# Leftover rows stacked by transfers, power-based guards and code products on GpSimd, in a spectral filter beside a product-key expert layer

## The chip, the cores and the metric

The kernel runs on one core of one Trainium2 chip. Its engines work side by side, each through its own instruction queue in order: TensorE (PE; its weight loads are listed apart as PEld), VectorE (DVE), ScalarE (ACT), GpSimd (POOL) and SyncE (SP), which here only issues DMA transfers. The metric is the time of one execution in microseconds on the device; the span in a profile is the part of it from the first to the last instruction.

## What is computed

`x` is 2048 tokens of 576 numbers, and `xn` its layer norm. The output is `x + A(xn) + B(xn)`:

```python
def _A_ref(x, w_r, w_i):                      # a filter in the frequency domain
    X = rfft2(x, axes=(-2, -1))               # over the 2048 tokens and the 576 columns
    return irfft2(X * (w_r + 1j * w_i), s=(S, D))

def _B_ref(x, w_q, k1, k2, u, v):             # 32 heads, 8 x 8 experts, the best key of each half
    q = einsum("nd,dhc->nhc", xf, w_q)        # w_q: 576 x 32 x 256
    s1, s2 = q[..., :128] @ k1.T, q[..., 128:] @ k2.T        # 8 scores each
    e = argmax(s1) * 8 + argmax(s2)           # one expert per token and head, its softmax weight is 1
    act = gelu(einsum("nd,nhkd->nhk", xf, u[e]))
    return einsum("nhk,nhk,nhkd->nd", 1, act, v[e])
```

## The kernel before

**Transform.** The 2048 tokens lie as 128 partitions by 16 tiles, so the token transform splits into a part of 64 points and one of 32. Each tile's 576 columns are folded into a sum half and a difference half of 289 columns (`folds`), of which 256 are the main columns and 33 are "leftovers". `dft128` multiplies both with the 64-point matrix `Rs` (scaled by the token's 1/sigma). float16 products need high and low parts: the main columns go to `AB` (high, low), and the leftovers to `ABL`, stacked three times on 99 partitions (33 low, 33 high, 33 high), so that one product does all three combinations. The stack is made beforehand: `folds` copies the 33 columns three times into `fl`, and PE repeats the work on 99 columns.

Then come 16 groups `g` of frequencies. `d_fwd(g)` does the column transform (12 products from `AB` and 2 from `ABL`), `s_fwd` the 32-point transform of a pair of groups, `s_mul` the filter weights `W` (loaded by `load_w`, scaled by `w_scale`), and `s_inv(g)` the inverse 32-point transform back into `AB` and `ABL`, again with the leftovers tripled through a copy `yl`. At the end, for 16 token tiles `t`, `d_inv(t)` does the inverse column transform and `fin` the 64-point one, adds the expert part (`CAT` times the high and low parts of `vS`, four products for each tile) and `x`, and stores.

**Experts.** `w_q` (18.9 MB, 32 transfers into the five buffers `w`) is folded with the keys as it arrives (`fold_part`), centred and split (`fold_end`, `fold_last`) into `MU` and `MUL`. In eight rounds `r` of 256 tokens, `x_t` loads and splits the transposed x (`xT`), `scores` does 28 products of 512 columns, takes the maximum over seven key differences, marks its place and multiplies the marks with a code of powers of two; `route` reduces the codes and forms the expert's one-hot parts; `combine` brings the coefficients into `CAT`.

**Guards.** So that float16 does not overflow, `allmax` finds the largest entry of a tensor (a transpose on PE, a maximum on DVE, a product on PE that broadcasts it) and scales by it. It serves `x_scale`, `uv_prep`, `w_scale` and `fold_scale`.

**Order.** The program text is only a list of operations, numbered as it is read, and matmuls of one stage are joined into operations of some 2000 array cycles. `ORDER` (line 134) gives the sequence in which all of them are issued, and `BANK` the PSUM bank of each tile; both were written by a planner. All instructions are issued at line 312, so the profile names the groups by their tiles: `Rs,A` is dft128's main part and `Rs,yl` its leftovers, `c,AB` and `c,ABL` are d_fwd and d_inv, `A,s` is s_fwd, `s,y` and `s,yl` are s_inv, `A,c` and `vS,MT` are fin, `MU,xT` and `MUL,xT` are scores, `w,KP` is fold_part, `c,wm`, `c,uv` and `c,mm_` are the transposes of `allmax`. `port` marks operations of DVE with more than one SBUF input and those of POOL with inputs; a marked POOL operation waits for the last marked DVE operation issued before it (line 315).

The functions that the change touches:

## Time and profile before

| | us |
|---|---|
| median of three runs | 209.82 (207.26 to 209.93) |
| the profiled execution | 209.11 |
| its span | 206.3 |
| PE busy | 195.5 (95%) |
| DVE busy | 172.8 (84%) |
| ACT busy | 120.7 (59%) |
| POOL busy | 97.6 (47%) |
| DMA moved | 43.4 MB, 210 GB/s on average |

The page has the busy time of each engine, the span in 40 slices (tenths of the slice), the chain of work that ended last, and groups of equal instructions with their total busy time, the mean duration of one in ns and the idle time of the engine just ahead of them. Matmul ends are modelled: they overlap, so a group's mean duration is longer than its share of PE. A timeline line gives start, duration, engine, operation and count.

### The profile page before, as it was taken

The page shows a single profiled execution, that of the slowest core. Times are in us where ns is not written, and L with a number is a line of the kernel's source. Part 1 is how long each engine was busy: PE and PEld are TensorE (multiplying, and loading weights), DVE is VectorE, ACT ScalarE, POOL GpSimd, SP SyncE. Part 2 cuts the span into 40 slices and gives each one's busy share as a digit, 9 for nine tenths or more (in the row PEclk, how much of TensorE's full clock was granted, in tenths as well). Part 3 has the DMA queues.
Part 4 walks back from the last instruction along what each step waited for, and adds up shares of the span by engine and source line. Part 5 has one row for each costly group of instructions (what it writes and reads, how often), then busy time and mean ns, then how long its engine had stood idle before and what let it go on. Part 6 is the DMA issues. An engine that isn't in the chain of part 4 may idle for free.

```text
span 206.3 us, 5748 instructions
## 1 busy us (share of the span) xinstructions
PE 195.5 (95%) x2239; PEld 134.3 (65%) x2239; DVE 172.8 (84%) x397; ACT 120.7 (59%) x272; POOL 97.6 (47%) x160
## 2 busy tenths in 40 slices
PE   7588999999998999999999999999999999999992
PEld 2388669786567658544556668565686667868850
DVE  2899898847485787659999999999999999999863
ACT  2799997842437629988686936608682432333400
POOL 4548464002250033179538227405176666959750
PEclk9999999999999999999999999999999999999999
DMA  6999899999999999554725502520000000123195
GB/s 209 394 416 420 308 381 412 403 407 374 376 380 410 335 371 318 176 178 129 280 67 174 211 0 79 165 102 5 0 3 0 0 3 0 62 114 118 65 362 206
DMA packets 14859, 43.39 MB, mean 210 GB/s; under 512 B 1904, under 2 KB 4720, under 8 KB 14576
## 3 DMA queue, kind: packets, MB, share of 16 engines
q1 hardware_dynamic: 14832, 43.03, 56.6%
q8 instruction: 17, 0.28, 0.6%
q14 instruction: 10, 0.08, 0.1%
HBM read 38.30 MB, written 4.72 MB: 209 GB/s over the span
## 4 chain that ended last, share of the span: by engine, by line
PE 84%; DMA 8%; DVE 4%; ACT 1%; issue 1%; POOL 1%; DVEq 0%; SPq 0%; ACTq 0%
PE banks L312 84%; DMA w<-in_wq_dram 6%; DVE A L312 2%; DMA XN<-in_x_dram 1%; DVE st L312 1%; DVE rr L312 1%; ACT t L312 0%; POOL A L312 0%; DVE AB L312 0%; POOL MUL L312 0%; DVE XN L312 0%; ACT rr L312 0%; POOL rr L312 0%; DVEq L1022 0%; ACT yl L312 0%
## 5 line engine op out<-in xcount | busy, mean ns | idle before, releaser
L312 PE MATMUL banks<-MU,xT 128*128 128x512 f16 x192 | 46.3, 379 | 0.0
L312 POOL TENSOR_TENSOR y<-t,t 128x289 f32<-128x289 f32 x32 | 21.5, 695 | 43.8 <-DVE t L312 21.6
L312 PEld LDWEIGHTS <-AB 128*128 128x128 f16 x400 | 33.9, 122 | 6.2 <-issue 1.9
L312 PEld LDWEIGHTS <-xT 128*128 128x128 f16 x224 | 21.3, 100 | 22.8 <-issue 0.9
L312 PE MATMUL banks<-c,AB 128*128 128x145 f16 (+1 forms) x384 | 35.1, 227 | 0.0
L312 POOL TENSOR_TENSOR xT<-xf,xT 128x640 f16<-128x640 f32 x16 | 22.8, 1433 | 24.4 <-DVE w L312 10.4
L312 DVE SCALAR_TENSOR_TENSOR t<-banks,wx,Wt 128x578 f32<-128x578 f32 x32 | 24.4, 812 | 7.1 <-PE banks L312 4.1
L312 POOL TENSOR_TENSOR A<-t 128x289 f32<-128x289 f32 x32 | 21.5, 694 | 7.0 <-DVE MT L312 3.8
L312 DVE TENSOR_TENSOR AB<-banks,AB 128x512 f16<-128x512 f32 x32 | 21.2, 675 | 1.8 <-ACT AB L312 1.7
L312 PE MATMUL banks<-Rs,A 64*128 64x128 f32 x256 | 18.6, 288 | 3.9 <-ACT Rs L312 2.9
L312 ACT ACTIVATE es<-banks,sc 128x290 f32<-128x290 f32 (+1 forms) x16 | 9.9, 625 | 18.9 <-PE banks L312 12.5
L312 PEld LDWEIGHTS banks<-Rs,A 64*128 64x128 f32 x256 | 16.5, 194 | 6.3 <-ACT Rs L312 4.6
L312 PE MATMUL banks<-w,KP 128*32 128x288 f32 x256 | 18.6, 412 | 1.3 <-DMA w<-in_wq_dram 1.2
L312 ACT ACTIVATE AB<-banks 128x512 f16<-128x512 f32 x32 | 18.4, 591 | 1.7 <-PE banks L312 1.2
L312 PE MATMUL banks<-c,ABL 99*128 99x289 f16 (+1 forms) x64 | 18.5, 290 | 0.0
L312 DVE TENSOR_REDUCE MT<-w 128x128 bf16<-128x896 bf16 (+1 forms) x16 | 18.2, 1140 | 0.1
L312 ACT ACTIVATE A<-banks 128x578 f32<-128x578 f32 x16 | 10.3, 645 | 13.1 <-PE banks L312 12.2
L312 PE MATMUL banks<-A,s 64*64 64x289 f32 x256 | 17.8, 410 | 0.0
L312 PE MATMUL banks<-s,y 64*128 64x128 f32 x256 | 17.4, 278 | 0.0
L312 ACT ACTIVATE ABL<-banks 99x256 f16<-99x256 f32 x32 | 11.6, 379 | 9.3 <-PE banks L312 8.8
L312 PEld LDWEIGHTS banks<-s,y 64*128 64x128 f32 x256 | 15.4, 187 | 2.1 <-issue 1.4
L312 DVE SCALAR_TENSOR_TENSOR XN<-banks,sc,XN 128x578 f32<-128x578 f32 (+1 forms) x18 | 12.9, 746 | 1.9 <-PE banks L312 1.9
(124 smaller groups left out, 359.9 us busy)
## 6 DMA issues: line engine op xcount, KB each, us to landing
w<-in_wq_dram SPq DMA_DIRECT2D x32, 576.0 KB, 6.9
xf<-in_xT_dram SPq DMA_DIRECT2D x16, 320.0 KB, 3.3
Wt<-in_W_dram SPq DMA_DIRECT2D x8, 578.0 KB, 6.6
out_dram<-XN SPq DMA_DIRECT2D x14, 288.0 KB, 2.4
s<-in_s_dram SPq DMA_DIRECT2D x16, 192.0 KB, 5.7
XN<-in_x_dram SPq DMA_DIRECT2D x2, 1156.0 KB, 12.6
XN<-in_x_dram SPq DMA_DIRECT2D x3, 578.0 KB, 5.8
c<-in_c_dram SPq DMA_DIRECT2D x1, 868.5 KB, 11.2
```

The lines of the kernel that those rows point to most:

```text
L312: o.last = fn(*[x.place() if isinstance(x, _Ps) else x for x in args], **{k: x.place() if isinstance(x, _Ps) else x for k, x in kw.items()})
```

## The change

- **Forward leftovers.** `folds` orders the columns so that 65 leftover columns of both halves lie side by side; `fl` and the copies go. `dft128` makes them once, high and low, in `HL`, and after the last tile `spread` fills the three rows of `ABL` with six transfers of 33 or 32 rows.
- **Inverse leftovers.** `s_inv` keeps the main columns. `s_left` does the leftovers of two groups in four quarters of the array and stacks them with six transfers; `s_last` does groups 14 and 15 as before, without transfers.
- In `d_fwd` and `d_inv` the leftover products come last and are operations of their own (`cut`).
- **Guards.** `root` replaces `allmax` except in `x_scale`: a sum of squares from ACT, one product on PE that adds over the partitions, and one DVE operation on the bit pattern that halves the exponent.
- **Codes.** Scores and codes lie with the seven differences outermost; the code product moves from DVE to POOL, and `route`'s reduction becomes three maxima.
- `CAT` holds high and low parts so that the low part of `vS` needs only half the rows; two such products of `fin` share the array. The tables `RT`, `_columns` halves and masks follow the new layouts, and `fold_last` writes chunk by chunk.
- `Rs` is scaled on POOL from tile 2 on; the statistics of tiles 10 and 14 move from DVE to ACT; three of four centrings in `fold_part` move from DVE to POOL; `EG` halves, so four of `d_inv`'s differences move from POOL to DVE. `y` and `es` share a buffer `U` with `HL`, and `y` gets four slots instead of two.
- `ORDER` and `BANK` are new throughout. In the new order on SP, two of spread's transfers stand ahead of the wq load numbered 331 and four behind it; on PE, the main products of groups 3, 0 and 1 come first, then that load's fold product, then the leftover product of group 1. The first `route` follows its code product at once on DVE; later ones have the next round's maximum and comparison between.

The diff, without `ORDER`, `BANK` and table construction:

```diff
+    def cut(self):
+        self.split = True
...
+    U = K([128, 2316], F32, "U")
+    slots["y"], slots["es"] = ([U[:, 579 * i:579 * i + 578] for i in range(4)], [U[:, 580 * i:580 * i + 580] for i in range(2)])
+    turn["y"] = turn["es"] = 0
+    HL = view(U, [64, 2, S], F16)
 
     ABg = AB.rearrange("p q c (g n) -> p q c g n", g=16)
     ABLg = ABL.rearrange("p b (g n) -> p b g n", g=16)
-    place = [8 * (g % 2) + g // 2 for g in range(16)]
+    place = [4 * (g % 4) + g // 4 for g in range(16)]
     ABt = AB.rearrange("p q c (n t) -> p q c n t", t=16)
     ABLt = ABL.rearrange("p b (n t) -> p b n t", t=16)
-    ABi = AB.rearrange("p q c (a g e m) -> p q (c a) g e m", a=2, g=16, e=2)
-    ABLi = ABL.rearrange("p b (a g e m) -> p (b a) g e m", a=2, g=16, e=2)
+    ABi = AB.rearrange("p q c (a e g m) -> p q (c a) g e m", a=2, g=16, e=2)
...
+    def root(src, k, dst, e):
+
+        p = PS("m", (128, 64))
+        P.matmul(p[:, :k], on[:, 0:1].to_broadcast([128, 128]), src, start=True, stop=True)
+        v = p[:, :k].bitcast(I32)
+        if len(dst.shape) == 3:
+            v = v.unsqueeze(2).to_broadcast([128, k, 2])
+        V.tensor_scalar(dst.bitcast(I32), v, 0.5, float(0x1FBD1DF5 + (e << 23)), op0=OP.mult, op1=OP.add)
+
+    SA = (3, 5, 7, 9, 10, 11, 13, 14, 15)
...
         xn = XN[:, t]
-        e = T([128, 2, L], F32, "e", 4, "A2")
-        G.tensor_tensor(e[:, 1], xn[:, 0:L], xn[:, L:], op=OP.subtract)
-        V.scalar_tensor_tensor(e[:, 0], xn[:, 0:L], rr[:, 2, t:t + 1], xn[:, L:], op0=OP.add, op1=OP.add)
+
+        e = T([128, 578], F32, "e", 4, "A2")
+        G.tensor_tensor(e[:, 0:256], xn[:, 31:287], xn[:, L + 31:L + 287], op=OP.subtract)
+        G.tensor_tensor(e[:, 256:287], xn[:, 0:31], xn[:, L:L + 31], op=OP.subtract)
+        V.scalar_tensor_tensor(e[:, 287:576], xn[:, 0:L], rr[:, 2, t:t + 1], xn[:, L:], op0=OP.add, op1=OP.add)
         Rs = T([128, 2, 64], F32, "Rs", 3)
-        A.activation(Rs, Rm, AF.Copy, scale=rr[:, 0, t:t + 1])
-        fl = T([128, 2, 3, 33], F32, "fl", 3, "yl")
-        if t in FG:
-            G.tensor_copy(fl, e[:, :, 0:33].unsqueeze(2).to_broadcast([128, 2, 3, 33]))
+        if t > 1:
+            G.tensor_scalar(Rs, Rm, rr[:, 0, t:t + 1], None, op0=OP.mult)
         else:
-            A.activation(fl, e[:, :, 0:33].unsqueeze(2).to_broadcast([128, 2, 3, 33]), AF.Copy)
-        FF[t] = (e, Rs, fl.rearrange("p b a k -> p b (a k)"))
+            A.activation(Rs, Rm, AF.Copy, scale=rr[:, 0, t:t + 1])
+        FF[t] = (e, Rs)
...
-        for b in range(2):
-            for h, r in enumerate(hs):
-                P.matmul(p[:99, h, 256 + 64 * b:320 + 64 * b], fl[r, b], Rs[r, 0], start=True,
-                         stop=True, tile_position=(64 * h, 0))
+        for h, r in enumerate(hs):
+            P.matmul(p[:65, h, 256:320], e[r, 256:321], Rs[r, 0], start=True, stop=True, tile_position=(64 * h, 0))
         m = p[:, :, 0:256].rearrange("p h (n r) -> p n h r", r=2)
-        l = p[:, :, 256:384].rearrange("p h (n r) -> p n h r", r=2)
+        l = p[:64, :, 256:320].rearrange("p h (n r) -> p n h r", r=2)
         hi, ab = (AB[:, q].rearrange("p c (h n) -> p (c h) n", n=64)[:, :, 4 * t:4 * t + 4].rearrange("p n (h r) -> p n h r", r=2)
                   for q in range(2))
         A.activation(hi, m, AF.Copy)
         V.tensor_tensor(ab, m, hi, op=OP.subtract)
-        lo = ABL.rearrange("p b (h n) -> p (b h) n", n=64)[:, :, 4 * t:4 * t + 4].rearrange("p n (h r) -> p n h r", r=2)
-        A.activation(lo[:99], l[:99], AF.Copy)
-        V.tensor_tensor(lo[:33], l[:33], lo[:33], op=OP.subtract)
+        lh, ll = (HL[:, q].rearrange("p (h n) -> p h n", n=64)[:, :, 4 * t:4 * t + 4].rearrange("p n (h r) -> p n h r", r=2)
+                  for q in range(2))
+        A.activation(lh, l, AF.Copy)
+        V.tensor_tensor(ll, l, lh, op=OP.subtract)
+
+    @staged
+    def spread():
+        for k, q in ((1, 0), (2, 0), (0, 1)):
+            for b, n in enumerate((33, 32)):
+                Q.dma_start(ABL[n * k:n * k + n, b], HL[31 * (1 - b):31 * (1 - b) + n, q])
...
-        V.tensor_reduce(uv[:, 0:1], uf, axis=AX, op=OP.max, apply_absolute_value=True)
-        V.tensor_reduce(uv[:, 1:2], vs, axis=AX, op=OP.max, apply_absolute_value=True)
-        allmax(uv[:, 0:2], 2, sc[:, 0:2])
+        for k, z in enumerate((uf, vs)):
+            A.activation(vS[:, 0, :z.shape[1]], z, AF.Square, accum_out=uv[:, k:k + 1])
+        root(uv[:, 0:2], 2, sc[:, 0:2], 1)
+        V.tensor_scalar(sc[:, 0:2], sc[:, 0:2], 1e-10, None, op0=OP.max)
...
-            if (b, s) == (3, 3):
-                V.tensor_reduce(mm_[:, 3 + h:4 + h], mt[b][:, h, :288], axis=AX, op=OP.max, apply_absolute_value=True)
...
+            A.activation(w[:, 0:2], mt[b][:, :, :288], AF.Square, accum_out=mm_[:, b:b + 1])
             V.tensor_scalar(c, c, -1.0 / 576, None, op0=OP.mult)
-            V.tensor_scalar(M, M, c, None, op0=OP.add)
+            (G if b < 3 else V).tensor_scalar(M, M, c, None, op0=OP.add)
             A.activation(MTL[:, b], M[:, 512:576].unsqueeze(1).to_broadcast([128, 2, 64]), AF.Copy)
-            if b < 3:
-                V.tensor_reduce(mm_[:, b:b + 1], M, axis=AX, op=OP.max, apply_absolute_value=True)
...
-        sv = p[:, :, :448].rearrange("p t (m e) -> p t m e", e=7)
+        sv = p[:, :, :448].rearrange("p t (e m) -> p t e m", e=7)
         mx = T([128, 2, 64], F32, "mx", 4)
-        V.tensor_reduce(mx, sv, axis=AX, op=OP.max)
+        V.tensor_reduce(mx, sv.rearrange("p t e m -> p t m e"), axis=AX, op=OP.max)
         wk = T([128, 2304], BF, "wk", 5, "w")
-        eq = wk[:, 0:896].rearrange("p (t m e) -> p t m e", t=2, e=7)
-        V.tensor_tensor(eq, sv, mx.unsqueeze(3).to_broadcast([128, 2, 64, 7]), op=OP.is_equal)
-        V.tensor_tensor(wk[:, 896:1792].rearrange("p (t n) -> p t n", t=2), wk[:, 0:896].rearrange("p (t n) -> p t n", t=2),
+        eq = wk[:, 0:896].rearrange("p (t e m) -> p t e m", t=2, e=7)
+        V.tensor_tensor(eq, sv, mx.unsqueeze(2).to_broadcast([128, 2, 7, 64]), op=OP.is_equal)
+        G.tensor_tensor(wk[:, 896:1792].rearrange("p (t n) -> p t n", t=2), wk[:, 0:896].rearrange("p (t n) -> p t n", t=2),
                         wt.unsqueeze(1).to_broadcast([128, 2, 448]), op=OP.mult)
...
-        wv = wk[:, 896:1792].rearrange("p (m e) -> p m e", e=7)
+        wv = wk[:, 896:1792].rearrange("p (t e m) -> p t e m", t=2, e=7)
...
-        V.tensor_reduce(v0, wv, axis=AX, op=OP.max)
+        V.tensor_tensor(wv[:, :, 4:7], wv[:, :, 4:7], wv[:, :, 0:3], op=OP.max)
+        V.tensor_tensor(wv[:, :, 3:5], wv[:, :, 3:5], wv[:, :, 5:7], op=OP.max)
+        V.tensor_tensor(v0.rearrange("p (t m) -> p t m", t=2), wv[:, :, 3], wv[:, :, 4], op=OP.max)
...
-        A.activation(chl[:, :, 0:64], ca, AF.Copy)
-        G.tensor_tensor(chl[:, :, 64:128], ca, chl[:, :, 0:64], op=OP.subtract)
+        c4 = chl.rearrange("p i (a e) -> p (i a) e", a=2)
+        A.activation(c4[:, 0:4:3], ca, AF.Copy)
+        G.tensor_tensor(c4[:, 1:3], ca, c4[:, 0:4:3], op=OP.subtract)
...
-            P.matmul(p[:, b, :L], ABLg[:99, b, place[g], :], dl[:99, b, :], start=True, stop=False)
             for c in range(2):
                 cs = slice(0, 145) if b == c else slice(145, 289)
                 for n, (ha, hb) in enumerate(((0, 0), (0, 1), (1, 0))):
-                    P.matmul(p[:, b, cs], ABg[:, ha, 2 * b + c, place[g], :], dc[:, b, hb, cs], start=False,
-                             stop=(c == 1 and n == 2))
+                    P.matmul(p[:, b, cs], ABg[:, ha, 2 * b + c, place[g], :], dc[:, b, hb, cs], start=(c == n == 0), stop=False)
+        plan.cut()
+        for b in range(2):
+            P.matmul(p[:, b, :L], ABLg[:(99, 96)[b], b, place[g], :], dl[:(99, 96)[b], b, :], start=False, stop=True)
...
-        yl = T([128, 2, 3, 33], F32, "yl", 3)
-        A.activation(yl, y[:, :, 128:161].unsqueeze(2).to_broadcast([128, 2, 3, 33]), AF.Copy)
-        Y[g] = (y, yl.rearrange("p r a k -> p r (a k)"))
+        Y[g] = y
 
     @staged
     def s_inv(g):
 
         p = PS("c", (128, 2, 4, 128))
-        (y, yl), s = Y.pop(g), S32.pop(g)[:, 192:]
-        for c in range(3):
+        y, s = Y[g], S32[g][:, 192:]
+        for c in range(2):
             for ri in range(2):
                 for e in range(2):
                     r = slice(64 * e, 64 * e + 64)
-                    pe = e ^ g % 2
-                    if c < 2:
-                        lt, po = y[r, ri, 161 * c:161 * c + 128], p[:, pe, c, :]
-                    else:
-                        lt, po = yl[r, ri], p[:99, pe, 2, :]
-                    P.matmul(po, lt, s[r, 64 * ri:64 * ri + 128], start=(ri == 0), stop=(ri == 1),
-                             tile_position=(64 * e, 0))
+                    P.matmul(p[:, e ^ g % 2, c, :], y[r, ri, 161 * c:161 * c + 128], s[r, 64 * ri:64 * ri + 128],
+                             start=(ri == 0), stop=(ri == 1), tile_position=(64 * e, 0))
         hi, ab = (ABi[:, q, :, g] for q in range(2))
         pv = p[:, :, 0:2].rearrange("p e c (b a m) -> p (c b a) e m", b=2, a=2)
         A.activation(hi, pv, AF.Copy)
         V.tensor_tensor(ab, pv, hi, op=OP.subtract)
-        lv = p[:99, :, 2].rearrange("p e (b a m) -> p (b a) e m", b=2, a=2)
-        lo = ABLi[:99, :, g]
-        A.activation(lo, lv, AF.Copy)
-        V.tensor_tensor(lo[:33], lv[:33], lo[:33], op=OP.subtract)
-
-
-    EG = range(0, 16, 2)
+
+    @staged
+    def s_left(g):
+        p = PS("c")
+        for ri in range(2):
+            for q in range(2):
+                y, s = Y[g + q], S32[g + q][:, 192:]
+                for e in range(2):
+                    r, o = slice(64 * e, 64 * e + 64), 64 * (e ^ q)
+                    P.matmul(p[o:o + 64, q, :128], y[r, ri, 128:192], s[r, 64 * ri:64 * ri + 128], start=(ri == 0),
+                             stop=(ri == 1), tile_position=(64 * e, o))
+        h = T([128, 2, 4, 64], F16, "lo", 2)
+        hi, lo = (h[:, n].rearrange("p c (q m) -> p c q m", q=2) for n in range(2))
+        pv = p[:, :, :128].rearrange("p q (c m) -> p c q m", c=4)
+        A.activation(hi, pv, AF.Copy)
+        V.tensor_tensor(lo, pv, hi, op=OP.subtract)
+        for k, n in ((1, 0), (2, 0), (0, 1)):
+            for e in range(2):
+                to = ABL[33 * k:33 * k + 33].rearrange("p b (a e n) -> p (b a) e n", a=2, e=2)
+                Q.dma_start(to[:, :, e, 32 * g:32 * g + 64], h[64 * e:64 * e + 33, n])
+
+
+    @staged
+    def s_last(g):
+
+        y, s = Y[g], S32[g][:, 192:]
+        yl = T([128, 2, 3, 33], F32, "lo", 2)
+        A.activation(yl, y[:, :, 128:161].unsqueeze(2).to_broadcast([128, 2, 3, 33]), AF.Copy)
+        p = PS("c")
+        for ri in range(2):
+            for e in range(2):
+                r = slice(64 * e, 64 * e + 64)
+                P.matmul(p[:99, e ^ g % 2, :128], yl[r, ri].rearrange("p a k -> p (a k)"), s[r, 64 * ri:64 * ri + 128],
+                         start=(ri == 0), stop=(ri == 1), tile_position=(64 * e, 0))
+        to = ABL[:99].rearrange("p b (a e g m) -> p (b a) g e m", a=2, e=2, g=16)[:, :, g]
+        pv = p[:99, :, :128].rearrange("p e (c m) -> p c e m", c=4)
+        A.activation(to, pv, AF.Copy)
+        V.tensor_tensor(to[:33], pv[:33], to[:33], op=OP.subtract)
+
+    EG = range(0, 16, 4)
...
+        for h in range(2):
+            for i in range(2):
+                r = slice(64 * i, 64 * i + 64)
+                P.matmul(ps[i][:, h, :L], CAT[r, t + i, :], vS[r, 1, L * h:L * h + L], start=False, stop=False,
+                         tile_position=(64 * i, 0))
         plan.pack = set()
         for i in range(2):
             for h in range(2):
-                for q in range(2):
-                    P.matmul(ps[i][:, h, :L], CAT[:, t + i, :], vS[:, q, L * h:L * h + L], start=False, stop=(q == 1))
+                P.matmul(ps[i][:, h, :L], CAT[:, t + i, :], vS[:, 0, L * h:L * h + L], start=False, stop=True)
...
+    spread()
...
+        if g > 13:
+            s_last(g)
+        elif g % 2:
+            s_left(g - 1)
         if g + 2 < 16:
             s_mul(g + 2)
         if g + 4 < 16:
             d_fwd(g + 4)
-            load_s32(g + 4)
             if g % 2 == 1:
+                load_s32(g + 3)
+                load_s32(g + 4)
```

80 lines of the change are left out of this document (44 added, 36 removed), and 127 rows, old and new, of tables (BANK, ORDER).

## The prediction

> **What bounds the kernel now.** I read the page first: its slices of the span and the chain.
>
> ```profile
> PE   7588999999998999999999999999999999999992
> DVE  2899898847485787659999999999999999999863
> DMA  6999899999999999554725502520000000123195
> PE 84%; DMA 8%; DVE 4%; ACT 1%; issue 1%; POOL 1%; DVEq 0%; SPq 0%; ACTq 0%
> ```
>
> TensorE (PE) is busy from the fifth slice on, VectorE (DVE) from the nineteenth, and the DMA engines are full for the first fifteen (a slice is 5.16 us). The chain in order of time:
>
> ```profile
> 22.65 6.62 DMA w<-in_wq_dram
> 29.32 27.28 PE banks L312 x407
> 56.61 6.03 DMA w<-in_wq_dram
> 62.68 139.31 PE banks L312 x1438
> ```
>
> and the engines by stretches (busy PE, PEld, DVE, ACT, POOL; clock, DMA share, GB/s):
>
> ```profile
> 10.00:20.00 10.00, 8.21 (x136) 7.87 (x137) 9.61 (x29) 10.00 (x29) 6.27 (x18) 1.00 1.02 420
> 30.00:40.00 10.00, 10.00 (x178) 8.90 (x176) 8.83 (x24) 8.00 (x21) 2.71 (x8) 1.00 1.03 412
> 105.00:120.00 15.00, 15.00 (x156) 9.42 (x157) 14.76 (x33) 11.66 (x21) 7.67 (x9) 1.00 0.41 135
> 165.00:180.00 15.00, 15.00 (x150) 10.69 (x149) 14.61 (x28) 4.69 (x11) 11.24 (x19) 1.00 0.06 22
> ```
>
> Three regimes. Up to about 30 us the normalisation is held by DVE and ScalarE (ACT), with the x and wq loads behind. From 30 to 202 us PE has no gap, although the wq loads fill the DMA to the fifteenth slice. In the late part DVE is within 2 or 3% of full, so it is a second bound just behind PE. Hence an edit is worth the PE time that it removes after 30 us, provided DVE falls by as much. The profiled execution took 209.1 us (span 206.3 and 2.8 around it), 0.7 under the median of 209.8; I sum against 209.1.
>
> **PE terms.** The rows:
>
> ```profile
> L312 PE MATMUL banks<-Rs,yl 64*99 64x64 f32 x128 | 7.5, 241 | 0.0
> L312 PE MATMUL banks<-s,yl 64*99 64x128 f32 x128 | 9.3, 269 | 0.0
> L312 PEld LDWEIGHTS banks<-A,s 64*64 64x64 f32 x256 | 9.9, 133 | 6.7 <-issue 1.3 <-ACT A L312 0.9 <-DVE w L312 0.4
> 30.00:40.00 10.00, 2.64 (x48) 2.51 (x48) 0.00 (x0) 1.34 (x4) 1.00 1.03 412
> 30.99 0.49 PE L312 MATMUL banks<-Rs,yl 64*99 64x64 f32 x8
> 31.31 1.18 PE L312 MATMUL banks<-Rs,A 64*128 64x128 f32 x16
> 42.29 0.27 PE L312 MATMUL banks<-c,wm 128*2 128x128 f32 x1
> 42.40 0.29 PE L312 MATMUL banks<-c,ABL 99*128 99x289 f16 x1
> 44.72 2.18 PE L312 MATMUL banks<-A,s 64*64 64x289 f32 x32
> 46.83 2.15 PE L312 MATMUL banks<-w,KP 128*32 128x288 f32 x32
> 65.19 1.04 PE L312 MATMUL banks<-s,yl 64*99 64x128 f32 x16
> 66.17 0.30 PE L312 MATMUL banks<-c,ABL 99*128 99x289 f16 x1
> 188.60 1.21 PE L312 MATMUL banks<-A,c 64*64 64x289 f32 x16
> 189.74 0.67 PE L312 MATMUL banks<-vS,MT 128*128 128x289 f16 x4
> 190.24 0.29 PE L312 MATMUL banks<-c,ABL 99*128 99x290 f16 x1
> ```
>
> A float32 matmul leaves two records. Ends are modelled, so I price a burst from its start to the next start.
>
> Forward leftovers (dft128): the 128 records become 64, because one product of 65 columns replaces two of 99. A tile's eight records take 31.31 - 30.99 = 0.32 us; halved, 0.16 less. Six of the 16 tiles (48 of 128 records) lie after 30 us: **-1.0**. The other ten save 1.6 that counts only where DVE and ACT let the front move; that is in the front's term below.
>
> Inverse leftovers (s_inv to s_left): 16 records take 66.17 - 65.19 = 0.98 us, that is 61 ns each and 7.8 us for 128. Afterwards 112 records run in four quarters of the array, as the s_fwd burst does: 32 records of 289 columns in 46.83 - 44.72 = 2.11 us, 66 ns each, 29 ns when scaled to 128 columns. The weight loads of that burst take 9.9/256 = 39 ns, which may be the floor. So 112 x 29 to 39 = 3.2 to 4.4, and s_last's 16 at 61 ns add 1.0: saved 2.4 to 3.6, taken **-2.8**, nearer the load row.
>
> Output (fin): four vS products take 190.24 - 189.74 = 0.50 us. The 32 that carry the low part become 32 of half height, two side by side: 32 x 125 ns = 4.0 becomes 2.0, **-2.0** (0 if the pairs do not overlap; the float32 rows of 64 partitions above do).
>
> Guards: ten transposes go (w_scale seven, uv one, fold_scale two) at 42.40 - 42.29 = 0.11 us each, **-1.1**; one matmul each stays. If a neighbour's fill hid them, 0. A DVE reduction goes with each; nothing waits longer.
>
> New switches of array layout: 16 records of fin's first step take 1.14 us from start to start, where sixteen at 66 ns would be 1.06. So leaving the quartered layout costs up to 0.1. s_left enters and leaves it seven times, s_last and fin's half-height products add some ten changes: 0 to 2.4, taken **+1.2**. The Trainium skill, TensorEngine Tiling (Array Packing), Key Properties, speaks against the change here: altering the tiling mode drains TensorE. It has no price; by that rule the term stays positive, and the trace's 0.08 us agrees.
>
> **The front.** The statistics of two more tiles (10 and 14) go from DVE to ACT, Rs goes to GpSimd (POOL), the tripled leftover copies vanish, and the low subtraction shrinks:
>
> ```profile
> L312 DVE BATCH_NORM_STATS2 st<-XN 128x6 f32<-128x288 f32 x18 | 7.2, 438 | 2.2 <-DMA XN<-in_x_dram 2.2
> L312 DVE TENSOR_TENSOR ABL<-banks,ABL 33x256 f16<-33x256 f32 x32 | 12.5, 406 | 1.5 <-ACT AB L312 0.8 <-ACT ABL L312 0.5
> ```
>
> DVE loses 2 x 2 x 0.438 = 1.8, and half of 16 x 0.406 at most, 3.2, since the elements per partition halve: up to 5 us on an engine that is 88 to 96% busy in the two early stretches above. ACT gains two tiles' statistics, but loses 14 of the Rs scalings. x still has to arrive, so I take **-2.0** (bounds 0 and -5), with the ten tiles above in it.
>
> Against that stands spread(): the leftovers reach ABL only through six transfers, three copies of 65 rows of 4 KB, 0.8 MB. At 412 GB/s that is 2.0 us on a full DMA. SP issues them in order among the wq loads: in the new order the last four stand behind one more wq load, and the leftover product of group 1 stands right after that load's fold product. Everything behind it on PE waits, then s_fwd and s_mul. The landing is bounded by
>
> ```profile
> w<-in_wq_dram SPq DMA_DIRECT2D x32, 576.0 KB, 6.9
> out_dram<-XN SPq DMA_DIRECT2D x14, 288.0 KB, 2.4
> ```
>
> 0 (three main products of d_fwd and folds cover it) to 6.9; four of the six are 0.53 MB, 1.3 us behind that load: **+1.5**. The 42 small transfers of s_left fall mostly in the empty DMA and are read only by the last matmul of d_inv. I cost them at nothing; if that cover goes, the last pair costs one landing, 2.4. Groups 14 and 15 avoid it through s_last. ACT, 8.00 of 10 busy from 30 to 40 us and less full later, takes the new squares at nothing.
>
> **DVE and POOL, late.**
>
> ```profile
> L312 DVE TENSOR_TENSOR w<-w,wt 128x896 bf16<-128x896 bf16 x8 | 5.3, 660 | 0.1
> L312 DVE TENSOR_REDUCE MT<-w 128x128 bf16<-128x896 bf16 x8 | 8.6, 1076 | 0.1
> L312 DVE TENSOR_TENSOR w<-w,MT 128x512 bf16<-128x512 bf16 x16 | 6.5, 416 | 0.1
> L312 DVE SCALAR_TENSOR_TENSOR t<-banks,sc,es 128x288 f32<-128x288 f32 x8 | 4.1, 514 | 0.7 <-POOL A L312 0.5 <-ACT es L312 0.2
> L312 POOL TENSOR_TENSOR xT<-xf,xT 128x640 f16<-128x640 f32 x16 | 22.8, 1433 | 24.4 <-DVE w L312 10.4 <-DVE wt L312 4.5 <-DVE wx L312 3.6
> 98.73 1.54 DVE L312 TENSOR_TENSOR w<-MT,iv 128x512 bf16<-128x512 bf16 x1
> 105.65 0.42 DVE L312 TENSOR_TENSOR w<-MT,iv 128x512 bf16<-128x512 bf16 x1
> 98.58 1.40 POOL L312 TENSOR_TENSOR xT<-xf,xT 128x640 f16<-128x640 f32 x1 [0.88 <-ACT xf L312]
> ```
>
> DVE loses the code product (5.3), 16 low subtractions of s_inv for 9 (2.8), and gets three maxima of 384, 256 and 128 elements for each reduction; on the line through 512 and 896 elements (0.09 us and 0.64 ns an element) they take 0.76 against 1.08, 2.5 in all. The strided maximum and the comparison keep their element counts: nothing, with 1 us either way. EG halves, so four differences return from POOL to DVE: +2.1. Sum -8.5, above the 4.7 that PE saves late, so DVE stays behind PE: no term. POOL takes 8 products of 896 elements, at 1433/640 = 2.24 ns about 2.0 us each, 16 in all, on 50 to 75% busy.
>
> **Sum:** -1.0 - 2.8 - 2.0 - 1.1 + 1.2 - 2.0 + 1.5 = -6.2, so 202.9; **203.0 us**. Its own range is 199 to 207.
>
> **Rivals.**
> 1. *The front swallows it* (207.6). Scores cannot start before the wq stream ends, in the fifteenth slice, and spread's 2.0 us lengthen that stream. If PE runs dry before it, only late savings count: ten of 16 groups' leftovers -1.8, fin -2.0, guards -0.7, switches +1.0, and +2.0: -1.5, 207.6. For: the DMA share of 1.03. Against: PE has no gap from 30 us and several groups to draw on.
> 2. *DVE waits for POOL* (216.6, slower). Each route needs its code product from POOL, and it can sit behind an xT difference. The 98.73 row starts inside POOL's 98.58 operation, ends just after it, and takes 1.54 instead of 0.42. If DVE stands 2.0 us for each of eight products, that is 16 - 8.5 = +7.5 on an engine that is 98% busy. It eats PE's gain from 0.5 us of standing per product ((8.5 - 4.7)/8), and the kernel gets slower beyond 1.1. Against: in the new order the route after the first has another round's maximum and comparison between product and use. The Trainium skill, SBUF — State Buffer, Who interferes with whom, has the rule: a DVE operation with two SBUF inputs and a GpSimd operation that reads SBUF exclude each other for a whole instruction. The 98.73 row agrees.
> 3. *The front was the bound* (198.4). If the relief of DVE before 40 us comes through whole (-5) and spread hides (0): 209.1 - 1.0 - 5 - 2.8 - 2.0 - 1.1 + 1.2 = 198.4. For: DVE and ACT are at 9.61 and 10.00 of 10 from 10 to 20 us. Against: the DMA share of 1.02 there.
>
> **Numbers.** Forecast 0.58, rival 1 0.22, rival 2 0.10, rival 3 0.10. A measurement of this kernel tells about 2% from no change: 205.6 and 214.0. A tenth of the forecast case lies above 205.6: faster 0.52 + 0.10 = 0.62, same 0.28, slower 0.10. The range 197 to 210 leaves out rival 2 and the edges of 1 and 3.
>
> **What would show it.** Right: s_left records near 35 ns, no s,yl product outside groups 14 and 15, PE without gaps from 40 us, DVE clearly under PE late. Wrong: a wait of PE on a transfer into ABL at 40 to 50 us above 3 us (rival 1 when the wq stream then ends late), or route maxima that start long after the operation before them, released by POOL (rival 2). PE gaps late with DVE full would break the premise that PE is what ends last.

## The result: 3.7% slower

The changed kernel takes 216.57 us (214.67 to 217.34), the kernel before 208.69 (207.26 to 209.93): ratio 1.037, 95% interval 1.026 to 1.048. The forecast was 203.0, with 197 to 210 as its range. The profiled execution took 217.34 us (span 215.2). Its slices, in the order PE, DVE, clock, DMA:

```profile
PE   7678797994799999799999999999999999999990
DVE  3859859370046166378495899999999996999883
PEclk9979999999589999999999999999999999999999
DMA  6999899899987999875875203416012100005476
```

PE, nearly without a hole from the fifth slice on before, now has holes up to the seventeenth (a slice is 5.4 us), the deepest in the tenth; from there it is full as before. So the loss lies in the first 92 us. Three rows from PE's timeline of the kernel before (last burst of `dft128`, first of scores, last of `fin`), then the same places in the changed kernel:

```profile
37.27 0.83 PE L312 MATMUL banks<-Rs,yl 64*99 64x64 f32 x16
...
83.86 1.03 PE L312 MATMUL banks<-MU,xT 128*128 128x512 f16 x4
...
201.55 0.67 PE L312 MATMUL banks<-vS,MT 128*128 128x289 f16 x4
```

```profile
40.01 1.56 PE L324 MATMUL banks<-Rs,A 64*128 64x128 f32 x28 [0.41 <-POOL Rs L324]
...
96.96 1.90 PE L324 MATMUL banks<-MU,xT 128*128 128x512 f16 x8
...
209.12 1.03 PE L324 MATMUL banks<-vS,MT 64*128 64x289 f16 x8
```

Scores start 13.1 us later (96.96 - 83.86), and the stretch from there to the last product is 5.5 us shorter (209.12 - 96.96 = 112.2 against 117.7). The difference is the 7.6 us that PE ends later. The late part is what the change was expected to bring; the front ate it and more.

Where PE stands still between 44 and 62 us, on PE and on SP's queue:

```profile
49.00 0.69 PE L324 MATMUL banks<-w,KP 128*32 128x288 f32 x8 [0.33 <-DMA w<-in_wq_dram]
49.62 0.94 PE L324 MATMUL banks<-c,AB 128*128 128x145 f16 x12
52.38 0.69 PE L324 MATMUL banks<-w,KP 128*32 128x288 f32 x8 [1.82 <-DMA w<-in_wq_dram]
54.87 1.71 PE L324 MATMUL banks<-c,ABL 99*128 99x289 f16 x6 [1.79 <-DMA ABL<-U]
```

```profile
42.64 1.26 SPq L324 DMA_DIRECT2D ABL<-U  x2
43.99 0.52 SPq L324 DMA_DIRECT2D w<-in_wq_dram  x1
44.57 3.17 SPq L324 DMA_DIRECT2D ABL<-U  x4
...
54.14 2.11 SPq L324 DMA_DIRECT2D w<-in_wq_dram  x4
```

`ABL<-U` are the transfers of `spread`. PE waits first for the wq load that was issued at 43.99 between them (it lands at 52.38, 8.4 us later), then for the rows themselves (issued until 47.74, there at 54.87). The next four wq loads go out at 54.14. By the profile it isn't a fold on PE that holds them: SP's waits just before end when the wq load lands (1.9 us) and then when rows of `spread` do. Its waits for such rows in the whole run (total, times, longest):

```profile
SPq L324 <- DMA ABL<-U: 1.6, 4, 0.6
```

### The profile page after: what moved, and what is told of

It is laid out like the page before. It is cut to its first block, busy times and chain, and to the rows that moved or that the text cites. A ratio compares the mean times of both kernels' runs of the same rounds, so it can differ in the third digit from the quotient of the medians.

```text
span 215.2 us, 5686 instructions
## 1 busy us (share of the span) xinstructions
PE 195.1 (91%) x2165; PEld 127.2 (59%) x2165; DVE 155.9 (72%) x379; ACT 115.4 (54%) x258; POOL 121.5 (56%) x184
## 5 line engine op out<-in xcount | busy, mean ns | idle before, releaser
L324 POOL TENSOR_TENSOR U<-t,t 128x289 f32<-128x289 f32 x32 | 21.7, 696 | 34.5 <-DMA xf<-in_xT_dram 23.3
L324 PE MATMUL banks<-Rs,A 64*128 64x128 f32 (+1 forms) x320 | 21.9, 289 | 7.1 <-POOL Rs L324 4.0
L324 PEld LDWEIGHTS banks<-Rs,A 64*128 64x128 f32 (+1 forms) x320 | 20.3, 195 | 11.6 <-POOL Rs L324 7.1
L324 PE MATMUL banks<-s,U 64*128 64x128 f32 (+1 forms) x368 | 21.7, 281 | 0.3
L324 PEld LDWEIGHTS banks<-s,U 64*128 64x128 f32 (+1 forms) x368 | 18.3, 170 | 5.7 <-issue 3.4
L324 POOL TENSOR_TENSOR A<-XN 128x31 f32<-128x31 f32 (+1 forms) x32 | 13.5, 438 | 5.8 <-DMA XN<-in_x_dram 2.1
L324 ACT ACTIVATE U<-banks,sc 128x290 f32<-128x290 f32 (+1 forms) x16 | 8.9, 565 | 12.9 <-PE banks L324 8.4
L324 DVE SCALAR_TENSOR_TENSOR t<-banks,sc,U 128x290 f32<-128x290 f32 (+1 forms) x28 | 13.7, 550 | 2.6 <-ACT U L324 1.8
L324 PE MATMUL banks<-c,ABL 99*128 99x289 f16 (+1 forms) x64 | 13.8, 306 | 1.8 <-DMA ABL<-U 1.8
L324 POOL TENSOR_TENSOR w<-w,wt 128x896 bf16<-128x896 bf16 x8 | 15.2, 1899 | 0.4 <-DVE MT L324 0.4
```

The source lines that it names most:

```text
L324: o.last = fn(*[x.place() if isinstance(x, _Ps) else x for x in args], **{k: x.place() if isinstance(x, _Ps) else x for k, x in kw.items()})
```

## The experiments

Theory **A**: the hand-over through `spread` holds up the front. **B**: DVE waits for the code product on POOL (the prediction's second rival). **C**: POOL, with `Rs`, paces the front. **D**: the new order itself. Times are medians; ratios are against the kernel before, run on the same chip.

### Without spread (A)

```diff
-                Q.dma_start(ABL[n * k:n * k + n, b], HL[31 * (1 - b):31 * (1 - b) + n, q])
-            P.matmul(p[:, b, :L], ABLg[:(99, 96)[b], b, place[g], :], dl[...], ...)
+            P.matmul(p[:, b, :L], ABg[:(99, 96)[b], 0, b, place[g], :], dl[...], ...)
```

> The six transfers of spread are left out, and the forward leftover products read a ready tile (AB) in place of ABL, so that the stacking itself is not computed; all else is the changed kernel (216.6 us). Theory A (the hand-over of the forward leftovers through spread makes PE stand near 50 to 55 us, halves its clock for the 6.8 us after it, and delays the wq stream): 207 to 210 us, no gap of PE above 1 us between 46 and 62 us, granted clock 1.00 there. Theory B (DVE standing for GpSimd's code products in the late part is the cause, rival 2 of the prediction): 215 to 217, since nothing late changes.

210.49 us, ratio 1.010 (1.003 to 1.017), just above A's range. Some 6 of the 8 us are `spread` (5.5 by the ratios); some 2 are not. In its trace scores start at 91.20, 5.8 us earlier than with it, and the four wq loads of 54.14 go out from 46.39 on (the profiled execution took 213.4 us, 2.9 above the median, so only its first half is used here).

```profile
91.20 1.90 PE L330 MATMUL banks<-MU,xT 128*128 128x512 f16 x8
```

### spread kept, but nobody reads its rows

The edit is the second half of the one above.

> The changed kernel with spread's six transfers left in, but with the forward leftover products reading AB instead of the rows that spread fills (as in the run without spread), so nothing waits for them and the forward leftovers are wrong. If PE's wait for the landing is the cost (with the half clock after it): 210 to 211.5 us, as without spread. If the cost is what the transfers take from the wq stream (shared DMA engines, 4.7 us of SP's issuing): 214 to 217 us.

214.78 us, ratio 1.030 (1.025 to 1.034). So two thirds of the 6 us are there without any wait of PE for the rows: 4.0 us (1.9% between this ratio and the one without `spread`). The wait itself adds what is left, 1.5 us by the ratios, which their intervals don't separate from nothing. The traces divide it otherwise. Scores start at 94.03 here, 2.8 us after 91.20 and 2.9 before 96.96:

```profile
94.03 1.90 PE L324 MATMUL banks<-MU,xT 128*128 128x512 f16 x8
```

How the 6 us divide is therefore known only to a microsecond or two. What the transfers do to the loads shows in the stretch 47 to 54.2 us: first without `spread`, then with the unread one (sum, busy PE, PEld, DVE, ACT, POOL; clock, DMA share, GB/s).

```profile
47.00:54.20 7.20, 6.57 (x90) 4.55 (x93) 1.25 (x10) 3.96 (x11) 0.00 (x0) 1.00 1.02 386
```

```profile
47.00:54.20 7.20, 4.97 (x60) 3.26 (x60) 1.14 (x9) 1.75 (x6) 0.00 (x0) 1.00 0.95 243
```

The DMA engines are as full as ever and move 243 GB/s in place of 386. Over 7.2 us that is 1.03 MB less. If 0.5 MB (the four later transfers) to all 0.8 MB of `spread` moved in it, 1.6 to 1.8 MB of loads are displaced, by this estimate 4.0 to 4.7 us at 386 GB/s. By its bytes alone `spread` would be 2.1 us.

### The transfers issued from another queue

```diff
-                Q.dma_start(ABL[n * k:n * k + n, b], HL[...])
+                A.dma_start(ABL[n * k:n * k + n, b], HL[...])     # second kernel: G.dma_start
```

> Only the queue of spread's six transfers changes, from SP to ACT. If the cost is that they stand in order among the wq loads on SP (4.7 us of issuing, and loads behind them), ABL is ready earlier, the gaps of PE at 49 to 54 us shrink under 1 us each and the wq loads are issued without a hole: 209 to 212 us. If the cost is the transfers themselves (0.8 MB in 4 KB rows that take the DMA engines from the wq stream for some 9 us), whoever issues them: gaps and half clock stay, 214 to 218 us.

> The changed kernel with spread's six transfers issued from GpSimd's queue, which has nothing to do at 44 to 63 us, instead of SP's. Without a reader they still cost 4.3 us (214.8 against 210.5), and the reader's wait 1.8 more. If those 4.3 us are SP's issuing (the wq loads behind them on SP start late): 211 to 213 us and no hole in SP's wq loads at 44 to 54 us. If they are the transfers' use of the shared DMA engines: 215 to 217 us.

From ACT 224.10 us, ratio 1.077 (1.070 to 1.085); from POOL 220.28, 1.060 (1.056 to 1.064). Both are worse, and above what either theory had expected of them. ACT first, then POOL, each with PE's wait:

```profile
53.40 2.36 ACTq L324 DMA_DIRECT2D ABL<-U  x3
...
63.70 0.40 PE L324 MATMUL banks<-c,ABL 99*128 99x289 f16 x1 [11.76 <-DMA ABL<-U]
```

```profile
44.83 3.25 POOL L324 DMA_DIRECT2D ABL<-U  x6 [4.82 <-DVE U L324]
...
56.77 0.40 PE L324 MATMUL banks<-c,ABL 99*128 99x289 f16 x1 [6.00 <-DMA ABL<-U]
```

On ACT the last transfers stand behind copies of PE's results that wait for PE, and go out until 55.76. On POOL all six are out by 48.08, and SP sends the next four wq loads from 46.03 on instead of 54.14. Yet the rows land 7.9 and 8.7 us after the last issue, as they land 7.1 us after it from SP. So the late landing isn't SP's queue; what the three have in common is the DMA engines, full of loads that are already queued (a DMA share of 1.02 from 47 to 54.2 us in the POOL run). The Trainium skill says so in DMA: Bandwidth & Descriptors, Issuing engines are not separate DMA queues: whichever engine starts a transfer, it runs on the same 16 engines, and only the time to issue it is saved. These two runs agree: POOL saved SP's issuing, and PE's wait for the rows grew from 1.79 to 6.00 us. How much of the 4.0 us above is the shared engines and how much SP's late issue isn't separated: an unread `spread` from POOL's queue was not run.

### PE's gaps filled

```diff
+            for _ in range(fill.get(i, 0)):           # fill = {332: 14, 484: 14}
+                P.matmul(p[:, 1, :L], zz, dc[:, 0, 0, :], start=False, stop=False)
```

> 28 products with a zero weight tile are put into the two places where PE stands between 50 and 55 us (14 each, added into a sum that is open there), nothing else; they cost PE about 3.6 us in time that it would stand. If the half clock from 54 to 61 us follows from PE standing: clock 1.00 there and 212 to 214 us. If the clock drops for another reason or its loss is made up later: 216 to 219.

216.0 us, ratio 1.038 (1.032 to 1.044). The filler was meant for the clock. In the changed kernel it is halved twice:

```profile
13.30:16.70 3.40, 3.40 (x38) 3.40 (x38) 1.27 (x7) 2.31 (x7) 1.67 (x6) 0.50 0.99 411
...
54.20:61.00 6.80, 6.13 (x44) 3.82 (x48) 0.15 (x1) 3.89 (x8) 0.00 (x0) 0.50 1.00 381
```

With 28 products by a zero weight in the two gaps the clock is 1.00 from 54.2 to 61 us, and the time stays within what the runs scatter. So the second half clock is not where the time went. The first, from 13.3 us, is left as it was (the clock from 10 to 25 us is 0.89 with the filler too), and what it costs was not tested. The two stretches are 3.4 and 6.8 us long. The Trainium skill, TensorE: Matmul & The Clock Gate, HAM oscillation, has a window of about 3.4 us after which an idle TensorE is throttled. The stretches are one and two such windows long, but PE's waits ahead of the second were shorter, 1.82 and 1.79 us with one burst of 0.69 between, so no run here shows the rule as it stands.

### The code product back on DVE (B)

```diff
-        G.tensor_tensor(wk[:, 896:1792]...
+        V.tensor_tensor(wk[:, 896:1792]...
```

> The code product goes back from GpSimd to DVE, nothing else. Theory B: DVE no longer stands for GpSimd, 208 to 212 us. Theory A: the late part is bound by PE and DVE has 5.3 us more to do there while it is 98% busy from 120 to 165 us: 216 to 220.

218.43 us, ratio 1.050 (1.044 to 1.056). Nothing comes back. By itself that doesn't settle B, because DVE, full in the late part, takes on the products again (5.3 us for eight, in the kernel before). The changed kernel's own rows settle it: DVE waits only 3.2 us for the products of POOL in eight rounds, so B falls as the cause of the 8 us.

```profile
L324 POOL TENSOR_TENSOR w<-w,wt 128x896 bf16<-128x896 bf16 x8 | 15.2, 1899 | 0.4 <-DVE MT L324 0.4
...
L324 DVE TENSOR_TENSOR w<-w 128x384 bf16<-128x384 bf16 x8 | 3.0, 381 | 3.3 <-POOL w L324 3.2
```

This edit touches nothing ahead of the scores, so its trace also tells how far two executions of the same front lie apart. Its scores start 2.0 us earlier than the 96.96 above, and those of the run with the filler at 94.90:

```profile
94.95 1.90 PE L324 MATMUL banks<-MU,xT 128*128 128x512 f16 x8
```

### The front: Rs, statistics, and the order (C and D)

Rs back on ACT in the changed kernel; then its statistics of tiles 10 and 14 back on DVE; then its whole front as before, in the new order:

```diff
-        if t > 1: G.tensor_scalar(Rs, Rm, rr[:, 0, t:t + 1], None, op0=OP.mult)
+        A.activation(Rs, Rm, AF.Copy, scale=rr[:, 0, t:t + 1])
```

> Rs of tiles 2 to 15 goes back from GpSimd to ACT, nothing else. Theory C (GpSimd paces the front: PE waited 4.0 us for its Rs, its weight loads 7.1): 210 to 213 us, with the half-clock stretch near 13 to 17 us gone. Theory A: at most 2 us gained, 214.5 to 217, because the wait for spread and the wq stream stand behind it.

```diff
-    SA = (3, 5, 7, 9, 10, 11, 13, 14, 15)
+    SA = (3, 5, 7, 9, 11, 13, 15)
```

> The changed kernel with the statistics of tiles 10 and 14 back on DVE (as before), Rs still on POOL, same order. If ACT's added statistics are what delays the first transform (they cost 4.2 us in the old order): last dft128 2 us or more before 41.4 us, 213 to 215 us. If it is POOL's Rs (6 us in the old order) or the new order itself: last dft128 at 41 us or later, 216 to 218 us.

```diff
-        lh, ll = (HL[:, q]...           # spread() gone, Rs on ACT, SA as before
+        fl = T([128, 2, 3, 33], F32, "fl", 3, "yl")
+                P.matmul(p[:99, h, 256 + 64 * b:320 + 64 * b], fl[r, b], Rs[r, 0], ...)
```

> The forward leftovers as in the kernel before (tripled copy fl, products of 99 columns, Rs scaled on ACT, statistics of 7 tiles on ACT, no HL and no spread); everything else as changed: s_left, half-height products, root, codes, the new ORDER. Theory A (the whole loss is the front: products that wait for HL, transfers and POOL): the last dft128 burst comes near 38 us again, scores start at 84 to 87 us, the late gain of 5 us stays: 203 to 207 us. Theory D (the new ORDER itself delays the wq folds, with 32 more s_fwd records and more transfers on SP ahead of the scores): scores start at 90 us or later: 210 to 213 us.

222.02 us (1.069, 1.061 to 1.076), 216.01 (1.033, 1.025 to 1.041) and 216.41 (1.037, 1.029 to 1.046). The last `dft128` bursts, in this order (the third kernel has its leftovers in a burst of their own):

```profile
44.03 3.45 PE L324 MATMUL banks<-Rs,A 64*128 64x128 f32 x60 [0.76 <-ACT Rs L324]
```

```profile
39.00 1.56 PE L329 MATMUL banks<-Rs,A 64*128 64x128 f32 x28 [0.40 <-POOL Rs L329]
```

```profile
42.90 3.14 PE L328 MATMUL banks<-Rs,A 64*128 64x128 f32 x48 [1.49 <-ACT Rs L328]
45.87 1.19 PE L328 MATMUL banks<-Rs,U 64*99 64x64 f32 x24
```

C falls as it was put: with `Rs` on ACT the first transform ends later, not earlier, and the time of 222 us is above both forecasts. The order was made for `Rs` on POOL, so the run doesn't show that `Rs` costs nothing there. With the statistics back the last burst starts 1.0 us earlier; other traces with this front have it from 39.44 (no transfers at all) to 40.60 (the filler), so that isn't clear of scatter, and the time moves by nothing that the intervals show. And the old front without `spread` gains nothing in the new order: its transform ends at 47 us, its scores start at 95.80, and what the missing hand-over saves is lost. That start is what D had forecast (90 us or later), but the time is 3 us above D's range, and no run isolates the new order itself.

The reverse test: the kernel before, in its own order, with the two shifts together, with `Rs` alone, with the statistics alone.

```diff
-    SA, FG = (3, 5, 7, 9, 11, 13, 15), range(2, 16)
+    SA, FG = (3, 5, 7, 9, 10, 11, 13, 14, 15), range(2, 16)
-        A.activation(Rs, Rm, AF.Copy, scale=rr[:, 0, t:t + 1])
+        if t > 1: G.tensor_scalar(Rs, Rm, rr[:, 0, t:t + 1], None, op0=OP.mult)
```

> The kernel before with the front's two shifts alone, in its own order: statistics of tiles 10 and 14 on ACT instead of DVE, Rs scaled on POOL from tile 2 on. The prediction's step (DVE bounds the front, its relief comes through): last dft128 burst 1 to 2 us before 37.9 us, 206 to 207 us. The other theory (the front is a chain through PE, ACT, DVE and POOL in which no engine is the bound, and POOL's Rs of 0.67 us adds a hand-over): last dft128 at 38 us or later, 208 to 210 us.

> The kernel before with one of the two front shifts alone: Rs scaled on POOL from tile 2 on, in the old order. If this hand-over is what cost b2_front its 12.8 us: 217 to 222 us, last dft128 at 46 us or later. If the statistics are the cause: 208 to 211 us.

> The kernel before with the other shift alone: statistics of tiles 10 and 14 on ACT instead of DVE, in the old order. If DVE bounds the front: 206 to 208 us. If ACT, which is as full as DVE from 10 to 25 us, becomes the longer one: 210 to 216 us, last dft128 at 41 us or later.

221.30 us (1.062, 1.057 to 1.066), 214.16 (1.030, 1.025 to 1.036) and 212.37 (1.022, 1.017 to 1.027); the single shifts have two runs each. Each costs by itself, and together they cost somewhat more than their sum, 6.2% against 5.2. The last `dft128` bursts start at 49.86, 43.35 and 41.24 in place of 37.27, that is 12.6, 6.1 and 4.0 us later, and the scores at 96.74, 90.51 and 87.09, 12.9, 6.7 and 3.2 us later: what the first transform loses goes through to the time whole (12.8, 6.0 and 4.2 us). In the old order both shifts lose, in the new one so does `Rs` when it is moved back. Two parts of the relief of DVE that the prediction priced at -2.0 are thus a loss of 13 us in the old order; its third part, the smaller low subtraction, wasn't run alone.

### The stacking transfers of s_left

Left out in the changed kernel, alone and together with `spread`:

```diff
-                Q.dma_start(to[:, :, e, 32 * g:32 * g + 64], h[64 * e:64 * e + 33, n])
```

> The 42 stacking transfers of s_left are left out (their issue takes 0.82 us each on SP, 34 us in all), so the inverse leftovers of 14 groups are not in ABL and the output misses them. If they are hidden, as the prediction costed them: within 1 us of the changed kernel, 215.5 to 217.5 us. If SP's issuing delays wq and x loads, or the last product of d_inv waits for them: 1 to 3 us less, and scores start earlier than 96 us.

> The changed kernel without any stacking transfer: spread's six and s_left's 42 are left out, and both leftover products read AB instead of the stacked rows (so all leftovers are wrong, at the same PE work). Single omissions gave 210.5 (spread) and 215.1 (s_left) against 216.6, so by their sum 209. If that holds, the transfers are 7.5 of the 8 us lost, and PE's savings late only pay for the later front. Below 207.5: the two together cost more than alone, and the savings of the change show. Above 210.5: s_left's transfers cost nothing once spread is gone.

215.08 us, 1.035 (1.027 to 1.042), and 210.95, 1.011 (1.007 to 1.015). The 42 transfers cost nothing that these runs show: 210.95 with neither, 210.49 without `spread` alone. That holds in the new order, which sends them one to five at a time and late. The kernel before with half-height products, `root` in `w_scale` and `s_left` tells what it hangs on: first with each pair's six transfers issued as soon as the rows are made, then the same with the code product on POOL, then with the six moved behind to a later group:

```diff
+                    P.matmul(p[o:o + 64, q, 2, :], yq[r, ri, 128:192], sq[r, 64 * ri:64 * ri + 128], ...)
+                    plan.ops[-1].calls.append((nc.sync.dma_start, (to[...], h[64 * e:64 * e + 33, n]), {}))
```

> The kernel before, in its own order, with the late parts of the change: half-height vS products, root in w_scale, and the inverse leftovers in quarters of the array with their 42 stacking transfers (s_left; groups 14 and 15 as before). The front, the forward leftovers and the codes stay as before. If the late terms of the prediction hold without the front: b1 gave 207.1, s_left takes 2.8 off and its array switches 0.5 to 1 on: 204.5 to 205.5 us. If SP's issue time for the 42 transfers delays the loads: 206.5 us or more.

> As b3_left, with the code product on GpSimd too (in the slot of the order where DVE did it, codes laid out as before). If DVE is the second bound late, close behind PE: another 0.5 to 2 us less, 203 to 204.5 us. If PE alone bounds: as b3_left within 0.5 us. If DVE waits for POOL (the second rival): above b3_left by 1 us or more.

> As b3_left, but with each pair's six transfers moved behind on SP, to the operations of a later group, so that no wq, filter or table load stands behind transfers whose data isn't ready; groups 12 to 15 as before, without transfers; one more buffer for the 32-point tables. If the 26 us that b3_left lost are SP's order (its loads queued behind transfers that wait): 205 to 206.5 us. If the transfers cost by themselves: 210 us or more.

234.78 us (1.127, 1.122 to 1.133), 238.11 (1.142, 1.138 to 1.145) and 210.56 (1.013, 1.009 to 1.016). SP and PE of the first:

```profile
60.97 6.54 SPq L325 DMA_DIRECT2D ABL<-lo  x6
67.61 2.07 SPq L325 DMA_DIRECT2D w<-in_wq_dram  x4
```

```profile
73.39 3.11 PE L325 MATMUL banks<-w,KP 128*32 128x288 f32 x24 [5.32 <-DMA w<-in_wq_dram]
```

SP stands for 2.7 us, from 58.26 on, until the high rows are there, the six transfers and a wait for the low rows keep it for 6.5 us more, the next wq loads go out behind them, and PE stands. Later PE stands 4.8 us for a table load and 4.4 for the rows themselves. Moved behind, 24 of the 26 us are back, and scores start at 83.04 in place of 92.18 (the last run differs in more than that: groups 12 and 13 are as before, and there are more buffers). It is still some 3.5 us above the next kernel, which has no `s_left`. PE stands there 2.3 us for `y` from POOL, 1.3 for ACT and 0.7 for a table load, none of which the next kernel's trace has; why they arise is not settled.

With the product on POOL the old order loses 3.3 us more, and there theory B's wait does appear, three times as long as in the new order:

```profile
DVE MT L325 <- POOL w L325: 10.6, 5, 2.8
```

### Two small parts alone

```diff
-                    P.matmul(ps[i][:, h, :L], CAT[:, t + i, :], vS[:, q, L * h:L * h + L], ...)
+                P.matmul(ps[i][:, h, :L], CAT[r, t + i, :], vS[r, 1, L * h:L * h + L], ..., tile_position=(64 * i, 0))
+                P.matmul(ps[i][:, h, :L], CAT[:, t + i, :], vS[:, 0, L * h:L * h + L], ...)
-        allmax(wm[:, g // 2:(g + n) // 2], n // 2, wx[:, 0, g:g + n]..., 256.0)
+        root(wm[:, g // 2:(g + n) // 2], n // 2, wx[:, 0, g:g + n]..., 13)
```

> The kernel before with two parts of the change alone, in its own ORDER: the 32 products with the low part of vS at half height in pairs, and the guard of w_scale by root (one product in place of a transpose, a maximum and a product). PE is without gaps late, so by the measured 89 ns in place of 125 the products save 1.2 us and seven transposes some 0.8: 206 to 207 us against 208.1 for the kernel before. If these terms are covered by something else late (DVE): 208.

207.07 us (206.29 to 208.54), ratio 0.995 (0.991 to 0.999). This is the kernel before, in its old order, with two parts that move nothing to another engine and need no transfer. It is faster than both kernels, by half a per cent against the one before.

## Why the prediction was wrong

**The regime was read rightly for the late part alone.** "From 30 to 202 us PE has no gap" was the ground for counting every microsecond of PE after 30 us. In the kernel before, PE already stood 1.0 us for wq loads between 30 and 202 us:

```profile
62.68 0.69 PE L312 MATMUL banks<-w,KP 128*32 128x288 f32 x8 [0.76 <-DMA w<-in_wq_dram]
```

It is the place where the prediction's own chain goes through a wq load. So up to the end of the wq stream PE was close to being held by loads, and in the changed kernel it has gaps up to 92 us. Late, PE and DVE are both full, and the terms come out so in the new order:

- *Inverse leftovers, -2.8.* Two bursts of `s_left`, with what follows each on PE:

```profile
140.36 0.67 PE L324 MATMUL banks<-s,U 64*64 64x128 f32 x16
140.84 2.13 PE L324 MATMUL banks<-A,s 64*64 64x289 f32 x32
...
154.62 0.61 PE L324 MATMUL banks<-s,U 64*64 64x128 f32 x16
155.17 2.33 PE L324 MATMUL banks<-MU,xT 128*128 128x512 f16 x10
```

  Sixteen records take 0.48 and 0.55 us, 30 to 34 ns each, where 29 to 39 was forecast; 112 take 3.4 to 3.9, and `s_last`'s sixteen 1.1 (from 174.17 to 175.29), as put.
- *Output, -2.0.* This was mis-sized. Eight `vS` products, four of them with the low part, go from 1.00 us to 0.87:

```profile
200.64 1.03 PE L324 MATMUL banks<-vS,MT 64*128 64x289 f16 x8
201.51 0.94 PE L324 MATMUL banks<-c,AB 128*128 128x145 f16 x12
```

  Eight such bursts save 1.0. Two products side by side don't take the time of one: with 0.50 for the four full ones, 0.37 is left for two pairs, where 0.25 was forecast.
- *Guards, -1.1.* Seven of the ten transposes and the output term together gave 1.0 us in the last experiment, where 0.8 of the forecast and the measured 1.0 were due; its interval (0.2 to 1.8) just holds that.
- *Switches, +1.2* were not measured apart.
- *DVE and POOL late.* DVE stays just under PE, as put (the stretch 120 to 165 us):

```profile
120.00:165.00 45.00, 44.88 (x450) 26.71 (x452) 44.02 (x105) 23.88 (x48) 27.56 (x30) 1.00 0.25 69
```

  The three maxima of a round take 381 + 287 + 222 = 890 ns, not 760.

Of the 5.5 us that the late part is shorter, some 2 are work that the new order does ahead of the scores. PE's groups between the first transform and the scores, before and after, show 32 more records of `s_fwd`, at the prediction's 66 ns each 2.1 us:

```profile
L312 PE MATMUL banks<-A,s 64*64 64x289 f32 x96 | 6.9, 410 | 0.0
```

```profile
L324 PE MATMUL banks<-A,s 64*64 64x289 f32 x128 | 9.9, 454 | 0.2 <-DMA s<-in_s_dram 0.2
```

That leaves 3.4, against 3.5 (rival 1's list without its transfer: -1.8 - 2.0 - 0.7 + 1.0). That the sum agrees is in part luck: the output gave 1.0 of its 2.0, so some other term, perhaps the switches, came out better than put.

**The step that failed most is "spread, +1.5".** It weighed a landing of 0 to 6.9 us and chose near its lower end. Measured, the rows land 7.1 us after the last issue, past the upper end, and by the estimate above the transfers displace twice their bytes, 4.0 to 4.7 us of loads. In all `spread` costs some 6 us, of which 4.0 by the ratios come without PE's wait. Rival 1 named the mechanism and the sign to look for; the wait for `ABL` that should have shown it is 1.79 us, below its mark of 3 and after its 40 to 50 us, because the wait for the wq load between the transfers took as much (1.82). Its price of +2.0, the bytes at full rate, was the error: scores start 3.7 to 5.8 us later by `spread` alone (91.20 against 94.95 and 96.96).

**The second is "the front, -2.0".** DVE's load did fall. Two stretches before, then after (columns as above):

```profile
10.00:25.00 15.00, 13.02 (x210) 10.90 (x210) 14.01 (x42) 14.92 (x44) 9.01 (x24) 1.00 0.97 382
25.00:40.00 15.00, 14.67 (x248) 12.21 (x248) 13.79 (x38) 12.60 (x33) 5.98 (x15) 1.00 1.01 399
```

```profile
10.00:25.00 15.00, 11.23 (x152) 9.41 (x152) 11.31 (x38) 12.94 (x38) 9.67 (x28) 0.89 0.95 372
25.00:40.00 15.00, 12.72 (x192) 10.05 (x192) 11.92 (x33) 12.22 (x35) 12.45 (x27) 1.00 0.96 357
```

DVE goes from 27.8 to 23.2 of 30 us, ACT from 27.5 to 25.2, and PE too falls behind: none of the three is full, nor is POOL (9.67 and 12.45 of 15), and the transform still ends later (the last burst ends at 41.6 in place of 38.1; one more wq load is folded by then, so the net is some 3 us). PE's standing ahead of the transform's products grew by as much, from 3.9 to 7.1 us, before and after:

```profile
L312 PE MATMUL banks<-Rs,A 64*128 64x128 f32 x256 | 18.6, 288 | 3.9 <-ACT Rs L312 2.9
```

```profile
L324 PE MATMUL banks<-Rs,A 64*128 64x128 f32 (+1 forms) x320 | 21.9, 289 | 7.1 <-POOL Rs L324 4.0
```

Before, 2.9 us of it were for `Rs` from ACT; now 4.0 are for `Rs` from POOL and 1.0 for the two that ACT still makes. POOL's `Rs` in turn waits 2.5 us for PE and 2.3 for ACT, and DVE from 8 to 42 us for ACT, POOL and PE, so the waits go round in a circle:

```profile
DVE rr L324 <- ACT rr L324: 2.2, 4, 1.1
DVE A L324 <- POOL rr L324: 1.5, 3, 0.9
DVE A L324 <- PE banks L324: 1.2, 1, 1.2
```

A share of 88 to 96% was read as "DVE is the bound, relief comes through". The runs fit a chain through four engines with in-order queues better, in which a moved operation shortens one link and lengthens another. Rival 3 falls with it. Why the new order is 3 us later is open in detail: `Rs` on POOL is its longest wait, but putting it back on ACT costs 5 us more by the medians, and the half clock from 13.3 us wasn't tested.

**The second rival gave the time (216.6) by coincidence and not the cause.** Its place, the route waiting for the product, shows 3.2 us in all where 16 were put, and without it the kernel is no faster.

Put together, for the start of scores: 5.8 by `spread`, 2.1 of work moved ahead, some 3 by the front; the remaining 2.2 of the 13.1 were not assigned. Since another trace of the same front starts its scores 2.0 us earlier, the parts are good to about 2 us, and the remainder may be scatter.

## What to carry to other kernels

Price a transfer inside a load stream by what it displaces and by the depth of what is already queued, not by its bytes at the best rate: here 0.8 MB between two SBUF tiles cost some 4 us without any reader, and landed 7 to 9 us after the last issue, whichever queue sent it. An engine that is 90% busy in a chain of short dependent steps isn't yet the bound: look at whether its waits, and those of its neighbours, go round, and don't count on relief unless the order is made for it. In an order written out by hand or by a planner, the one edit that moved no operation to another engine and added no transfer brought a gain, of about half what its rows said; those that did must be priced with the order.

## What was not expected of the hardware

Full DMA engines moved 243 to 250 GB/s while the 33-row transfers ran from SP's queue, 308 while they ran from POOL's, and 386 without them. SP needs 0.56 to 0.90 us to issue one of them (3.17 us for four in a row) and 0.82 to 1.01 for a stacking transfer of `s_left`; a wq load of 576 KB takes it 0.33 when nothing holds it up. The granted clock stayed at one half for 6.8 us after PE's two short waits at 50 to 55 us, though PE was busy again, and lifting it brought nothing that the runs show. SP, with transfers of its own in flight, stood until some of them had landed before it issued the next loads.
